# When the tile of probabilities is taken, which banks the transposes use, and which group's scores go first

## The chip, the cores and the metric

One core of a Trainium2 chip runs the kernel. The metric is the device time of one execution in microseconds; the figure of a kernel is the median of its runs. TensorE does the matmuls (row name PE, its weight loads PEld), VectorE (DVE), ScalarE (ACT) and GpSimd (POOL) do the rest, and SyncE (SP) issues most transfers.

## The reference

Three layers one after the other, in float32 (the weights come as 64-bit floats and are unpacked on the chip):

```
def _attn_ref(q, k, v):                    # 4 x 8 heads x 576 x 64
    scores = scale * np.matmul(q, k.transpose(0, 1, 3, 2))
    rel = pos[:, None] - pos[None, :]
    mask = (rel >= 0) & (rel < window)     # window = 64
    scores = np.where(mask, scores, -1000000000.0)
    attn = np.exp(scores - np.max(scores, axis=-1, keepdims=True))
    attn = attn / (np.sum(attn, axis=-1, keepdims=True) + 1e-09)
    return np.matmul(attn, v)

def _moe_ref(x, w_in, w_out):              # 2304 tokens, 512 -> 2048 -> 512
    h = x @ w_in
    return (h * (1.0 / (1.0 + np.exp(-1.702 * h)))) @ w_out

def _moe2_ref(x, w_gate, w_val, w_out, rms_g):   # 512 -> 1536 -> 512
    xn = x / np.sqrt(np.mean(x * x, axis=-1, keepdims=True) + 1e-06) * rms_g
    g = xn @ w_gate
    return (g * (1.0 / (1.0 + np.exp(-g))) * (xn @ w_val)) @ w_out
```

The output is the third applied to the second applied to the attention output, rearranged to 2304 tokens of 512.

## The kernel before

Every operand of the two feed-forward layers is split into a high and a low half that TensorE multiplies in its faster float32 form; three matmuls (high with high, high with low, low with high) stand for one.

**Groups.** Attention works on 36 groups of 64 tokens, all eight heads at once. A group `g` runs: scores on TensorE (`scores`, L428); scale and mask on VectorE into the tile of probabilities `e` (`masked`, L453); the row maximum (L458); exponentials on ScalarE in place, with the row sums (L463); the inverse of the sum (L468, L469); the product with it on GpSimd, in place (`normal`, L472); the transposes of four 128 x 128 blocks on TensorE (`turned`, L477); their copy out of the accumulator into `pt` or `pts` (`turned_out`, through the helper at L312 or L314); the products with v (`values`, L487); and the split of the result into `xh` and `xl` (L312, L494), columns of a ring that the next layer reads. Groups 0 to 7 (`g < NS`) use other tiles and run first. From group 18 (`g >= NPE`) on, VectorE and GpSimd do the transposes instead of TensorE.

**First feed-forward layer.** Six blocks of 512, 256, 384, 384, 384 and 384 tokens. A block runs 16 steps; step c multiplies x with the slab of `w_in` number 2c (the up product, 12 matmuls, L554 to L556), applies the gate with ScalarE (L607) and VectorE (L611), splits the result into `gh` (L312) and `gl` (L569), and multiplies with the slab of `w_out` number 2c + 1 (the down product, 12 matmuls, L628 to L630). In the first block the slabs are made as they are needed: a transfer (L336), ScalarE (L340), three steps on VectorE (L344, L348, L354), a copy as the high half (L312) and a subtraction as the low half (L381). In the program's names the slabs are slab_82 to slab_105, then late_1303 to late_1310: slab_82 is the up slab of step 0, slab_83 the down slab of step 0, slab_84 the up slab of step 1. The groups of attention for a block are spread over the steps of the block before it.

**Second feed-forward layer.** From about 490 us on, products L912 to L914 (with combinations on VectorE, L938) and L1013 to L1015.

**Who decides the order.** Everything is recorded in a `Planner` as operations with costs, priorities, read and written tiles and newly taken buffers (`new=`). `emit` goes through planned time and gives each engine the ready operation with the lowest priority number; where an operation may run on several engines (a subtraction on VectorE or GpSimd, a copy on ScalarE or VectorE), it also decides that. What it emits is each engine's fixed order on the chip. An operation that takes a buffer of a ring waits until the buffer's last user is through. The rings that matter here, in `KINDS`:

```
        "bank": (ps, 2, [P, 512], F32),
        "abank": (ps, 2, [P, 512], F32),
...
        "v": (at, 1, [P, DM], F32),
        "e": (at, 1, [P, NK, P], F32),
        "pt": (at, 1, [P, NK, P], F32),
```

`bank` holds up products; `abank` holds scores, value products and a block's sums; `e` and `pt` are single. `step`, an argument of `attention`, is added to the priority number of a group's transposes and all that follows them; the groups of blocks 2 to 5 stand 13/6 apart in priority, those of block 1 13/4.

Of the kernel before, what the change touches and what calls it, by code (L numbers as in the profile page):

```python
# [189 lines left out]
def act(n, sbuf=True, extra=0):  # L190
    return n / 1200.0 + (0.093 if sbuf else 0.05) + 0.093 * extra


def dve(n, fast=False):
    return n * (0.52e-3 if fast else 1.042e-3) + 0.068
# [11 lines left out]
def window_attention_two_moe_kernel(ctx: ExitStack, tc: tile.TileContext, ins, out):  # L207
# [20 lines left out]
    NPE = gbase[3]  # L228
    NS = ngrp[0]
# [60 lines left out]
    pl = Planner({k: v[1] for k, v in KINDS.items()})  # L290
# [100 lines left out]
    def wkey(g):  # L391
        b, i = divmod(g, NBLK)
        return b, max(i - 1, 0)

    def load_q(g, prio, kind="q"):
        b, i = divmod(g, NBLK)
        t = q_of[g] = Buf(kind)
        pl.op({"D": dma(P * 2048)}, lambda e: nc.sync.dma_start(out=make(t), in_=qh[b, i]), prio, new=[t])

    def load_k(g, prio, kind="k"):  # L400
        if wkey(g) in kw:
            return
        b, i = wkey(g)
        t = kw[b, i] = Buf(kind)
        pl.op({"D": dma(P * 2048)}, lambda e: nc.sync.dma_start(out=make(t), in_=kh[b, :, i:i + 2]), prio, new=[t])

    def load_v(g, prio, kind="v"):
        if wkey(g) in vw:
            return
        b, i = wkey(g)  # L410
        t = vw[b, i] = Buf(kind)
        pl.op({"D": dma(P * 2048)},
              lambda e: nc.sync.dma_start(out=make(t), in_=vh[b, i * W:(i + 2) * W]), prio, new=[t])
# [5 lines left out]
    def attention(g, p0, step, ekind="e", ptkind="pt", norm=("G",), ptev=("A", "V"), hi=("A",)):  # L419
        q, k, v = q_of.pop(g), kw[wkey(g)], vw[wkey(g)]  # L420
        sb, eb, nb, ub, rb = Buf(f"y{g % 3}" if g < NS else "abank"), Buf(ekind), Buf("nm"), Buf("su"), Buf("rc")
        tb, pb, ob = Buf("bank" if g < NS else "abank"), Buf(ptkind), Buf("abank")
        extra = [START] if ekind == "e0" or ptkind == "pt0" or q.kind == "q0" or k.kind == "k0" or v.kind == "v0" else []

        def scores(e):
# [72 lines left out]
        c = (g * W) % RING // W  # L498
        d = step
        if g < NS:  # L500
            pl.op({"T": 1.09}, masked_scores, p0, r=[q, k, "mask", "negative", "ident", *extra],
                  w=[("xh", c), ("xl", c), "scores order"], new=[sb])
            pl.op({"V": dve(512) + 0.1}, highest_of, p0, r=[sb], new=[nb])
            pl.op({"A": 4 * act(128, True, 2)}, powers_of, p0, r=[sb, nb, *extra], new=[ub, eb])
        else:
            pl.op({"T": 0.872}, scores, p0, r=[q, k, *extra], w=[("xh", c), ("xl", c), "scores order"], new=[sb, eb],
                  after=vals[NS - 1:NS] if g >= NS else ())
            pl.op({"V": dve(512)}, masked, p0, r=[sb, "mask"], w=[eb])
            pl.op({"V": dve(512)}, highest, p0, r=[eb], new=[nb])
            pl.op({"A": 4 * act(128, True, 2)}, powers, p0, r=[nb], w=[eb], new=[ub])  # L510
        pl.op({"V": 0.29}, inverse, p0, r=[ub], new=[rb])
# [89 lines left out]
    def a_up(j, c, prio):  # L601
        n = sizes[j]
        hb, o = up("h", lambda: slab_of(2 * c), ("slab", 2 * c), tok0[j], n, prio)
        tb = Buf("th")

        def squash(e):
            nc.scalar.activation(out=make(tb)[:, 0:n], in_=hb.tile[:, 0:n], func=AF.Tanh, scale=0.851)  # L607

        def gated(e):
            th = tb.tile[:, 0:n]  # L610
            nc.vector.scalar_tensor_tensor(out=th, in0=th, scalar=1.0, in1=hb.tile[:, 0:n],  # L611
                                           op0=ALU.add, op1=ALU.mult)

        pl.op({"A": act(n, False)}, squash, prio, r=[hb], new=[tb])
        pl.op({"V": dve(n)}, gated, prio, r=[hb], w=[tb])
        return split(tb, n, prio, tok0[j]), o
# [471 lines left out]
    for g in range(NS):  # L1088
        attention(g, -60 + g, 0.5, "e0" if g >= 2 else ("e", "t1")[g], "pt0" if g % 2 else "pt",
                  norm=("G",) if g < NS - 1 else ("V",))  # L1090
# [14 lines left out]
    order = sorted(range(2 * NA), key=lambda i: need[i])  # L1105
    for i in order:
        c = i // 2
# [18 lines left out]
    def a_down(s):  # L1126
        j, c = steps[s]
        if c == 0:
            accs[j] = [Buf(f"y{m}") for m in range(NK)]
        down_t(accs[j], gates.pop(s), lambda: slab_of(2 * c + 1), ("slab", 2 * c + 1), c == 0, c == NA - 1, sizes[j],  # L1130
               s + LAG)
        if c == NA - 1:
            a_finish(j, accs.pop(j), s + LAG)
# [17 lines left out]
    def b_narrow(i):  # L1151
        (kind, c), src, _ = b_list[i]
        p = n0 + i * (n1 - n0) / len(b_list)
        key = ("w32d", "o", c) if kind == "o" else ("w32d", c - c % 2 + "gv".index(kind), c % 2)
        w_narrow(key, src, p + 8, after=[ups[int(p) - 2]], apart=kind == "o", late=6.0)
        b = w32.pop(key)
        if kind == "o":
            pl.op({"D": dma(P * 2048)}, lambda e: nc.sync.dma_start(out=w32o_d[c], in_=b.tile), p + 8, r=[b], w=[key])
            return
        n = key[1]  # L1160
        if c % 2 == 0:
            halfway[n] = b
            return
        pair = (halfway.pop(n), b)

        def word(h, k, lane):
            return pair[h].tile[:, k * 256:(k + 1) * 256, lane].bitcast(F32)

        for to, x, y, op in (((0, 0), (1, 0, 1), (1, 1, 1), ALU.add), ((0, 1), (0, 0, 0), (0, 0, 1), ALU.subtract),
                             ((1, 0), (0, 0, 1), (1, 0, 1), ALU.subtract), ((1, 1), (0, 1, 1), (0, 1, 0), ALU.subtract)):  # L1170
            xs = [(n, "sum", *v[:2]) for v in (x, y) if v[2] == 0]
            fn = lambda e, to=to, x=x, y=y, op=op: eng[e].tensor_tensor(out=word(*to, 0), in0=word(*x), in1=word(*y), op=op)
            pl.op(both(256), fn, p + 8, r=[*pair, *xs], w=[(n, "sum", *to)], port="GV")
        for h in range(2):
            pl.op({"D": dma(P * 4096)}, lambda e, h=h: nc.sync.dma_start(
                out=w32p_d[n][:, h].bitcast(I32), in_=pair[h].tile), p + 8,
                r=[pair[h], (n, "sum", h, 0), (n, "sum", h, 1)], w=[("w32d", n, h)])
# [4 lines left out]
    for s in range(SA):  # L1182
        j, c = steps[s]
        while pi < len(plans) and plans[pi][0] <= s:
            p, g = plans[pi]
            pi += 1
            load_q(g, p - 4)
            load_k(g, p - 4)
            load_v(g, p - 3)
            attention(g, p - 0.3, 2)  # L1190
        gs, o = a_up(j, c, s)
        ups.append(o)
        gates[s] = gs
        if s - 2 in gates:
            a_down(s - 2)
        while bi < len(b_list) and n0 + bi * (n1 - n0) / len(b_list) <= s:
            b_narrow(bi)
            bi += 1
# [11 lines left out]
    for n in range(NBB * NU):  # L1210
# [4 lines left out]
        if n % 2:  # L1215
            q = n // 2
# [60 lines left out]
```

## Time and profile before

| | |
|---|---|
| runs | 925.57, 926.16 and 928.45 us; median 926.16 us |
| the profiled execution | 925.49 us, with a span of 923.7 us |
| TensorE (PE) busy in the span | 902.2 us, 98% |
| VectorE, ScalarE, GpSimd busy | 647.3, 438.4, 273.2 us |
| granted clock of TensorE, mean | 0.997 |

The span goes from the first to the last instruction of the program; the profiled execution's own time includes what lies around it. Busy shares are averages over stretches that are limited by different things; the rows below are from single stretches. In a row of a timeline stand start, duration, engine, line, operation, written tile <- read tiles, shapes, the number of instructions, and in brackets the idle time before it with what ended it. In a row of waits stand the waiting engine and line, who released it, the total, the number of waits and the longest.

### The profile page before, as it was taken

The numbers are of one execution on the slowest core, as the hardware profiler recorded it, in microseconds if no ns is written. First come the engines' busy times: TensorE is split into PE (matmuls) and PEld (weight loads), VectorE is DVE, ScalarE is ACT, GpSimd is POOL, SyncE is SP. The second block draws the span as 40 slices with busy tenths as digits, with TensorE's granted clock in tenths as the row PEclk, the third lists the DMA queues.
The fourth block names the chain that finished last, engine by engine and source line by source line (L and its number), as shares of the span: only waits on it lengthen the run. The fifth ranks groups of instructions, "written<-read, shape, count | busy, mean of one in ns | idle before, by whom it ended". The sixth has DMA issues, their size and how long they took to land.

```text
span 923.7 us, 15362 instructions
## 1 busy us (share of the span) xinstructions
PE 902.2 (98%) x5436; PEld 835.9 (90%) x5436; DVE 647.3 (70%) x1236; ACT 438.4 (47%) x1081; POOL 273.2 (30%) x387
## 2 busy tenths in 40 slices
PE   8899999999999999999999999999999999999998
PEld 7677789989999999999998989898999999999997
DVE  5999996676767667666467888778667556555553
ACT  6666665566566667565336444443322223322222
POOL 4111012334345342442102622334223225222210
PEclk9999999999999999999999999999999999999999
DMA  8655557665445656543366999888986768966741
GB/s 283 226 174 201 193 188 159 222 206 171 151 147 186 169 183 229 183 160 114 106 231 233 234 359 341 320 280 255 321 236 206 206 201 244 284 205 205 205 144 68
DMA packets 86536, 194.63 MB, mean 211 GB/s; under 512 B 12726, under 2 KB 36027, under 8 KB 84924
## 3 DMA queue, kind: packets, MB, share of 16 engines
q1 hardware_dynamic: 66108, 137.02, 44.5%
q0 software_dynamic: 20352, 56.63, 21.0%
q8 instruction: 43, 0.70, 0.3%
q14 instruction: 33, 0.27, 0.1%
HBM read 140.13 MB, written 53.50 MB: 210 GB/s over the span
## 4 chain that ended last, share of the span: by engine, by line
PE 77%; DVE 12%; DMA 6%; issue 2%; ACT 2%; SPq 0%; POOL 0%; DVEq 0%; ACTq 0%; POOLq 0%
PE bank L912 9%; PE bank L913 9%; PE bank L914 9%; PE y L628 5%; PE y L630 5%; PE y L629 5%; PE bank L554 5%; PE bank L555 5%; PE bank L556 5%; PE y L1013 3%; PE y L1015 3%; PE y L1014 3%; PE abank L428 3%; DVE raw L348 2%; PE abank L487 2%
## 5 line engine op out<-in xcount | busy, mean ns | idle before, releaser
L554 PE MATMUL bank<-xh,slab 128*128 128x384 f32 (+2 forms) x288 | 98.3, 341 | 1.0 <-DVE th L611 1.0
L628 PE MATMUL y<-gh,slab 128*128 128x384 f32 (+2 forms) x288 | 98.5, 342 | 0.5 <-DVE y L653 0.5
L556 PE MATMUL bank<-xh,slab 128*128 128x384 f32 (+2 forms) x288 | 97.0, 337 | 2.0 <-DVE slab L381 2.0
L555 PE MATMUL bank<-xl,slab 128*128 128x384 f32 (+2 forms) x288 | 97.3, 338 | 0.4 <-DVE xl L494 0.3
L630 PE MATMUL y<-gh,slab 128*128 128x384 f32 (+2 forms) x288 | 96.9, 337 | 0.5 <-DVE slab L381 0.5
L629 PE MATMUL y<-gl,slab 128*128 128x384 f32 (+2 forms) x288 | 96.6, 336 | 0.0
L951 ACT ACTIVATE sb<-gh 128x384 f32<-128x384 f32 x72 | 37.8, 525 | 114.0 <-DVE gh L938 114.0
L312 ACT ACTIVATE xh<-sb 128x384 fp32r<-128x384 f32 x72 | 37.1, 521 | 107.5 <-DVE sb L966 107.5
L938 DVE TENSOR_TENSOR gh<-gl,bank 128x384 f32<-128x384 f32 x108 | 59.3, 551 | 35.9 <-PE bank L914 35.1
L611 DVE SCALAR_TENSOR_TENSOR th<-th,bank 128x384 f32<-128x384 f32 (+2 forms) x96 | 52.7, 549 | 42.8 <-ACT th L607 42.3
L913 PE MATMUL bank<-slab,late 128*128 128x384 f32 x228 | 77.0, 338 | 0.0
L913 PE MATMUL bank<-slab,slab 128*128 128x384 f32 x228 | 76.4, 335 | 0.0
L607 ACT ACTIVATE th<-bank 128x384 f32<-128x384 f32 (+2 forms) x96 | 46.7, 486 | 58.1 <-PE bank L556 55.0
L472 POOL TENSOR_TENSOR e<-e,rc 128x512 f32<-128x512 f32 x34 | 37.8, 1111 | 108.9 <-DVE rc L469 102.8
L312 ACT ACTIVATE gh<-th 128x384 fp32r<-128x384 f32 (+2 forms) x96 | 50.2, 523 | 40.3 <-DVE th L611 31.3
L938 DVE TENSOR_TENSOR gl<-gl,bank 128x384 f32<-128x384 f32 x72 | 39.8, 553 | 35.4 <-PE bank L914 31.4
L463 ACT ACTIVATE e<-e,nm 128x128 f32<-128x128 f32 x112 | 43.7, 393 | 33.2 <-DVE nm L458 31.0
L556 PEld LDWEIGHTS bank<-xh,slab 128*128 128x128 f32 x288 | 54.1, 188 | 4.9 <-DVE slab L381 2.8
L554 PEld LDWEIGHTS bank<-xh,slab 128*128 128x128 f32 x288 | 54.1, 188 | 3.6 <-DVE th L611 1.6
L630 PEld LDWEIGHTS y<-gh,slab 128*128 128x128 f32 x288 | 54.1, 188 | 3.2 <-DVE slab L381 1.2
L555 PEld LDWEIGHTS bank<-xl,slab 128*128 128x128 f32 x288 | 54.1, 188 | 3.1 <-DVE xl L494 1.1
L912 PE MATMUL bank<-slab,slab 128*128 128x384 f32 x156 | 53.0, 340 | 3.8 <-ACT th L312 1.7
(198 smaller groups left out, 2596.9 us busy)
## 6 DMA issues: line engine op xcount, KB each, us to landing
slab<-wc POOLq DMA_DIRECT2D x36, 512.0 KB, 4.6
late<-wc POOLq DMA_DIRECT2D x36, 512.0 KB, 4.3
wp<-raw SPq DMA_DIRECT2D x24, 512.0 KB, 4.1
fw<-wp SPq DMA_DIRECT2D x12, 1024.0 KB, 8.1
late<-wo POOLq DMA_DIRECT2D x22, 512.0 KB, 5.5
q<-in_q_dram SPq DMA_DIRECT2D x36, 256.0 KB, 4.4
wc<-slab SPq DMA_DIRECT2D x18, 512.0 KB, 7.1
wc<-late SPq DMA_DIRECT2D x18, 512.0 KB, 5.7
```

The source lines that it names most:

```text
L312: nc.scalar.activation(out=out, in_=in_, func=AF.Copy)
L554: nc.tensor.matmul(h, w[:, 0, kk], xh_ring[:, kk, cols], start=(kk == 0), stop=False)
L555: nc.tensor.matmul(h, w[:, 0, kk], xl_ring[:, kk, cols], start=False, stop=False)
L556: nc.tensor.matmul(h, w[:, 1, kk], xh_ring[:, kk, cols], start=False, stop=(kk == NK - 1))
L611: nc.vector.scalar_tensor_tensor(out=th, in0=th, scalar=1.0, in1=hb.tile[:, 0:n], op0=ALU.add, op1=ALU.mult)
L628: nc.tensor.matmul(y, s[:, 0, cols], hb.tile[:, 0:n], start=first, stop=False)
L629: nc.tensor.matmul(y, s[:, 0, cols], lb.tile[:, 0:n], start=False, stop=False)
L630: nc.tensor.matmul(y, s[:, 1, cols], hb.tile[:, 0:n], start=False, stop=last)
L912: nc.tensor.matmul(h, w[:, 0, kk], xh[:, kk], start=kk == 0, stop=False)
L913: nc.tensor.matmul(h, w[:, 0, kk], xl[:, kk], start=False, stop=False)
L914: nc.tensor.matmul(h, w[:, 1, kk], xh[:, kk], start=False, stop=kk == 1)
L938: nc.vector.tensor_tensor(out=(make(to) if kind else s.tile)[:, 0:HT].bitcast(F32), in0=s.tile[:, 0:HT].bitcast(F32), in1=b.tile[:, 0:HT], ...
```

## The change

For groups from 8 on, three things. The tile of probabilities `e` is taken by the mask step, and no longer by the scores; since `e` is single, the scores of a group no longer wait for the transposes of the group before. The transposes of groups 8 to 17 take their accumulator from `bank`, the ring of two that the up products use, and no longer from `abank`. And `step` is 2.3 where it was 2, so that in the blocks whose groups stand 13/6 apart the next group's scores come ahead of a group's transposes.

```
     def attention(g, p0, step, ekind="e", ptkind="pt", norm=("G",), ptev=("A", "V"), hi=("A",)):
...
-        tb, pb, ob = Buf("bank" if g < NS else "abank"), Buf(ptkind), Buf("abank")
+        tb, pb, ob = Buf("bank" if g < NPE else "abank"), Buf(ptkind), Buf("abank")
...
-            pl.op({"T": 0.872}, scores, p0, r=[q, k, *extra], w=[("xh", c), ("xl", c), "scores order"], new=[sb, eb],
+            pl.op({"T": 0.872}, scores, p0, r=[q, k, *extra], w=[("xh", c), ("xl", c), "scores order"], new=[sb],
                   after=vals[NS - 1:NS] if g >= NS else ())
-            pl.op({"V": dve(512)}, masked, p0, r=[sb, "mask"], w=[eb])
+            pl.op({"V": dve(512)}, masked, p0, r=[sb, "mask"], new=[eb])
...
-            attention(g, p - 0.3, 2)
+            attention(g, p - 0.3, 2.3)
```

The planner then makes another order on every engine from the first of these groups until far into the second layer. Three places of it follow: two of the 512-token block and the 256-token block.

TensorE, the transposes of group 8, early in the 512-token block (`abank<-ident,e` and `bank<-ident,e` are the transposes, `abank<-pts,v` the value products of group 8, slab_86 the third up product, slab_83 the first down product):

```order
 L555 MATMUL bank<-xl,slab_84 128x512
 L556 MATMUL bank<-xh,slab_84 128x512
-L477 MATMUL abank<-ident,e 128x128 x4
+L477 MATMUL bank<-ident,e 128x128 x4
+L628 MATMUL y_710<-gh,slab_83 128x512
+L629 MATMUL y_710<-gl,slab_83 128x512
+L630 MATMUL y_710<-gh,slab_83 128x512
+L487 MATMUL abank<-pts,v 64x64 x8
 L554 MATMUL bank<-xh,slab_86 128x512
 L555 MATMUL bank<-xl,slab_86 128x512
```

The value products and the first three matmuls of the first down product now stand ahead of the third up product; before, both stood behind it.

GpSimd in the same block, before:

```order
L472 TENSOR_TENSOR e<-e,rc 128x512
L381 TENSOR_TENSOR slab_90<-raw,slab_90 128x512
L472 TENSOR_TENSOR e<-e,rc 128x512
L381 TENSOR_TENSOR slab_94<-raw,slab_94 128x512
L569 TENSOR_TENSOR gl<-th,gh 128x512
L472 TENSOR_TENSOR e<-e,rc 128x512
L381 TENSOR_TENSOR slab_99<-raw,slab_99 128x512
L472 TENSOR_TENSOR e<-e,rc 128x512
```

and in the change:

```order
L472 TENSOR_TENSOR e<-e,rc 128x512
L381 TENSOR_TENSOR slab_90<-raw,slab_90 128x512
L472 TENSOR_TENSOR e<-e,rc 128x512
L381 TENSOR_TENSOR slab_96<-raw,slab_96 128x512
L381 TENSOR_TENSOR slab_98<-raw,slab_98 128x512
L472 TENSOR_TENSOR e<-e,rc 128x512
L381 TENSOR_TENSOR slab_97<-raw,slab_97 128x512
L381 TENSOR_TENSOR slab_102<-raw,slab_102 128x512
```

The low halves of slabs 96 and 98 have come to GpSimd, and that of slab 94 has gone to VectorE, with the one split of a gate (L569).

TensorE in the 256-token block: the change puts the scores of groups 13 and 14 on both sides of the value products of group 12, and the transposes of group 14 directly behind the scores of group 15 (`L685` and `L686` are the sums of the block before):

```order
L685 MATMUL abank<-gh,ones 128x512
L686 MATMUL abank<-gl,ones 128x512
L428 MATMUL abank<-k,q 128x128 x4
L487 MATMUL abank<-pts,v 64x64 x8
L428 MATMUL abank<-k,q 128x128 x4
L628 MATMUL y_1654<-gh,slab_87 128x256
```

And six products further on:

```order
L556 MATMUL bank<-xh,slab_94 128x256
L428 MATMUL abank<-k,q 128x128 x4
L477 MATMUL bank<-ident,e 128x128 x4
L554 MATMUL bank<-xh,slab_96 128x256
L555 MATMUL bank<-xl,slab_96 128x256
```

Before, a group's scores stood in this block behind the value products of the group before, with four products or more between a group's scores and its transposes.

At the end of the same block, before (late_1310 is its last down slab, `abank<-k,q` the scores of group 18, `128x384` the first up product of the next block):

```order
L628 MATMUL y_1683<-gh,late_1310 128x256
L629 MATMUL y_1683<-gl,late_1310 128x256
L630 MATMUL y_1683<-gh,late_1310 128x256
L477 MATMUL abank<-ident,e 128x128 x4
L628 MATMUL y_1690<-gh,late_1310 128x256
L629 MATMUL y_1690<-gl,late_1310 128x256
L630 MATMUL y_1690<-gh,late_1310 128x256
L487 MATMUL abank<-pts,v 64x64 x8
L428 MATMUL abank<-k,q 128x128 x4
L554 MATMUL bank<-xh,slab_82 128x384
```

and in the change (late_1306 is the down slab two steps earlier):

```order
L628 MATMUL y_1696<-gh,late_1306 128x256
L629 MATMUL y_1696<-gl,late_1306 128x256
L630 MATMUL y_1696<-gh,late_1306 128x256
L428 MATMUL abank<-k,q 128x128 x4
L554 MATMUL bank<-xh,slab_82 128x384
L555 MATMUL bank<-xl,slab_82 128x384
```

The transposes and value products of group 17 no longer stand here; the transposes now stand ahead of the up product with late_1305, the value products behind it.

## Rows read from the trace of the kernel before

**Rows 1.** Busy time by stretch: length, busy PE, PEld, DVE, ACT, POOL, clock, DMA.
```profile
32.00:130.00 98.00, 94.63 (x479) 74.76 (x480) 93.85 (x165) 63.32 (x131) 12.73 (x10) 1.00 0.55 187
...
187.00:203.00 16.00, 14.25 (x106) 12.81 (x105) 12.63 (x27) 11.25 (x37) 5.00 (x5) 1.00 0.67 223
203.00:424.00 221.00, 220.97 (x1524) 215.08 (x1522) 146.65 (x284) 139.66 (x411) 93.51 (x159) 1.00 0.51 170
```

**Rows 2.** Timeline of TensorE in the 512-token block, five places.
```profile
37.88 0.66 PE L477 MATMUL abank<-ident,e 128*128 128x128 f32 x4 [0.19 <-POOL e L472]
39.03 0.50 PE L554 MATMUL bank<-xh,slab 128*128 128x512 f32 x1 [0.49 <-DVE th L611]
...
45.51 1.05 PE L428 MATMUL abank<-k,q 128*128 128x128 f32 x8
...
55.83 0.50 PE L630 MATMUL y<-gh,slab 128*128 128x512 f32 x1 [0.46 <-DVE slab L381]
...
79.04 0.50 PE L556 MATMUL bank<-xh,slab 128*128 128x512 f32 x1 [1.34 <-DVE slab L381]
```

**Rows 3.** Timeline of VectorE at three places of the first 150 us.
```profile
38.30 0.67 DVE L611 SCALAR_TENSOR_TENSOR th<-th,bank 128x512 f32<-128x512 f32 x1
...
39.84 0.68 DVE L569 TENSOR_TENSOR gl<-th,gh 128x512 fp32r<-128x512 f32 x1
...
41.04 0.68 DVE L611 SCALAR_TENSOR_TENSOR th<-th,bank 128x512 f32<-128x512 f32 x1
...
77.46 1.53 DVE L381 TENSOR_TENSOR slab<-raw,slab 128x512 fp32r<-128x512 f32 x1
...
149.27 0.69 DVE L453 SCALAR_TENSOR_TENSOR e<-abank,m_rest 128x512 f32<-128x512 f32 x1 [0.24 <-PE abank L428]
```

**Rows 4.** Timeline of TensorE in the 256-token block, the starts of six pieces.
```profile
153.31 0.28 PE L628 MATMUL y<-gh,slab 128*128 128x256 f32 x1
...
154.73 0.60 PE L477 MATMUL abank<-ident,e 128*128 128x128 f32 x4
155.09 0.36 PE L554 MATMUL bank<-xh,slab 128*128 128x256 f32 x1
...
156.67 0.69 PE L487 MATMUL abank<-pts,v 128*64 128x64 f32 x16
157.29 1.16 PE L428 MATMUL abank<-k,q 128*128 128x128 f32 x8
158.20 0.36 PE L628 MATMUL y<-gh,slab 128*128 128x256 f32 x1
```

**Rows 5.** Timeline of ScalarE, the copy of group 8's transposes.
```profile
40.59 0.60 ACT L312 ACTIVATE pts<-abank 128x512 f32<-128x512 f32 x1
```

**Rows 6.** Timeline of GpSimd, the normalisation of groups 10 and 13.
```profile
77.13 1.31 POOL L472 TENSOR_TENSOR e<-e,rc 128x512 f32<-128x512 f32 x1 [3.15 <-DVE rc L469]
...
153.25 1.04 POOL L472 TENSOR_TENSOR e<-e,rc 128x512 f32<-128x512 f32 x1 [0.94 <-DVE rc L469]
```

**Rows 7.** Waits of TensorE from 130 to 187 us.
```profile
PE y L628 <- DVE y L653: 0.5, 1, 0.5
```

**Rows 8.** DMA issues: KB each, median us to landing.
```profile
v<-in_v_dram SPq DMA_DIRECT2D x32, 256.0 KB, 3.1
```

**Rows 9.** Waits of TensorE from 187 to 203 us.
```profile
PE bank L554 <- DVE th L611: 0.5, 1, 0.5
PE y L629 <- POOL gl L569: 0.5, 1, 0.5
PE abank L487 <- ACT pts L312: 0.4, 1, 0.4
PE abank L477 <- POOL e L472: 0.3, 1, 0.3
```

**Rows 10.** Waits of TensorE from 424 to 640 us, two of four.
```profile
PE bank L912 <- ACT th L312: 1.7, 1, 1.7
...
PE bank L912 <- DVE th L611: 1.0, 1, 1.0
```

## The prediction

> **What bounds the kernel now.** I read the profile in this order: busy time by stretch, then what TensorE waits for in each stretch, then the timeline around the waits.
>
> The stretches [rows 1] tell three stories. From 32 to 130 us (first layer, 512-token block, weights being unpacked) VectorE is busy 93.85 of 98 us and TensorE 94.63: two engines are full at once, and either can end a wait. From 203 to 424 us TensorE is busy 220.97 of 221: nothing that attention does there can be gained, only lost. Between them, from 187 to 203 us, TensorE is busy 14.25 of 16. That is the place to look at: it is the end of the 256-token block, where the first 384-token block wants x of groups 12 to 17.
>
> Below, S, T and V are a group's scores, transposes and value products on TensorE; U and D with a slab number are a first-layer up product and down product.
>
> **The change part by part.** No matmul and no DMA is added or removed; a few copies and subtractions go to another engine. What changes is what each step may wait for, and so the whole order. I cost it place by place.
>
> *1. T8 (a loss).* Before, T8 runs at 37.88 and U86 at 39.03 [rows 2]. In the change T8 takes a bank of the up products. That ring has two, which U82 and U84 hold, so T8 waits until U82's bank is read, by VectorE's step L611 that ends at 38.30 + 0.67 = 38.97 [rows 3]; VectorE's order is the same up to here in both builds. T8 takes 0.36 [rows 4], so it ends near 39.4. Next stand three matmuls of D83, which need the low half of the first gate, L569, ready at 39.84 + 0.68 = 40.52 [rows 3]. A product of twelve takes 1.42 at 256 columns [rows 4], so 2.84 at 512, and three matmuls 0.71: 40.6 to 41.3. V8 needs ScalarE's copy, done at 40.59 + 0.60 = 41.19 [rows 5]: no wait. V8 takes 0.62 [rows 4], to 41.9; U86's bank (U84's) is free at 41.04 + 0.68 = 41.72 [rows 3], no wait either. U86 2.84 and the nine remaining matmuls of D83 2.1 bring S9 to 46.85, where it stood at 45.51 [rows 2]: **+1.35**.
>
> *2. What the first stretch gives back.* It is full on VectorE too, and the two next waits there are for VectorE: 0.46 at 55.83 and 1.34 at 79.04 [rows 2]. TensorE arriving 1.35 late meets the first one already over. The second is for the low half of slab 98, L381 on VectorE, 77.46 to 78.99; it took 1.53 beside GpSimd's L472, 1.31 from 77.13 [rows 3, 6]. In the change GpSimd makes slabs 96 and 98, and VectorE makes slab 94 and takes group 10's mask and maximum later, so I expect slab 98 before it is asked for. A first matmul after other work lasts 0.36 where one in a run lasts 0.28 [rows 4], so each wait costs 0.1 more than its idle time. Both waits: -(0.46 + 1.34 + 0.2) = **-2.0**. Bounds: nothing (VectorE gives back none of it, its work is as much as before) to all of the stretch's 98 - 94.63 = 3.4 idle [rows 1].
>
> The Trainium skill, "SBUF — State Buffer", section "Who interferes with whom", says that a VectorE instruction with two SBUF inputs and a GpSimd instruction that reads SBUF exclude one another for the whole instruction, so that moving a subtraction to GpSimd frees VectorE of nothing while both run. The 1.53 beside GpSimd's 1.31 agrees. By that rule alone the 79.04 wait stays; that is a rival below.
>
> *3. Evacuation at 141 us.* One wait of 0.5 for VectorE's copy of an accumulator [rows 7]; the change gives three of these four copies to ScalarE and comes to the place one transpose later. I take **-0.5**; bounds -0.6 and 0.
>
> *4. New waits in the 256-token block.* S may now run while the probabilities before it are still in use, so S13, V12 and S14 stand in one row. S14 takes the accumulator bank that the mask step of S13 frees: 0.69 plus 0.24 of handover [rows 3], of which V12 covers 0.62 [rows 4]: +0.3. T14 stands directly behind S15. From the start of a group's mask step to the end of its normalisation is 153.25 + 1.04 - 149.27 = 5.02 [rows 3, 6]. The mask step of group 14 starts when T13 has read the one tile of probabilities; from there to T14 TensorE has U92 1.58, V13 0.62, U94 1.5 and S15 0.91 [rows 4], 4.61: +0.4. T15, T16 and T17 have three to five products between, 1.42 each [rows 4], and wait for nothing. SyncE's queue: the load of v for a group waits for V of the group before (one buffer) and lands in 3.1 [rows 8]; from V13 to V14 lie 1.5 + 0.91 + 0.4 + 0.36 + 1.58 = 4.7, so it is covered by over a microsecond; q and k go two groups ahead. Behind the waiting T14 stand U96 and V14 alone, and their users have slack of a product or more. In all **+0.7**; bounds 0 and +2.0 (each of S14, T13 to T17 waiting about 0.35).
>
> *5. The end of that block.* Before, D, T17, three matmuls of D, V17 and S18 stand in one knot in front of the 384-token block, and TensorE waits 0.5 for GpSimd's low half, 0.3 for GpSimd's normalisation, 0.4 for ScalarE's copy, and 0.5 for the bank of the third up product in a row [rows 9]: all of 187 to 203, 1.75 idle [rows 1]. In the change T17 and V17 stand five and six products earlier, and the up products of the new block alternate with the last down products, so that each bank has a product's time to be read. All four go, with 0.1 of restart each: **-2.1**. Nothing is late next: the x of group 17 is ready before U82.
>
> *6. Beyond 424 us.* The last wait of the first layer, 1.0 for VectorE's L611 at the first product of the second layer [rows 10], now has a down product more in front of it. The rest of the second layer's order on TensorE is the same; its VectorE and GpSimd shares are dealt anew. I take **-0.5**, bounds -2.0 and +2.0.
>
> Between 203 and 424 us I take nothing: TensorE has no idle time to give [rows 1], and a product there is half as long again as in the 256-token block, so the same chain of 5.02 has more cover.
>
> **Sum.** 1.35 - 2.0 - 0.5 + 0.7 - 2.1 - 0.5 = -3.05. The profiled execution took 925.49 us, so 922.4; it lies 0.67 under the median of the runs, 926.16, so I predict a median of **923.1 us**. About 0.3%, 2.8 us, is what a measurement of this kernel can tell from no change, so this is just beyond it. This case by itself spans 920 to 925.5.
>
> **The rivals.**
> *A, slower: the shared bank.* Each of the ten transposed groups puts its T between two up products, so an up product must wait for the gate step of the one right before it. At 38 us the bank came free 4.0 after U84's end (T8 followed it after 0.19 of idle time, so it ended at 37.69 [rows 2]; L611 at 41.72 [rows 3]), while T9 to T11 leave 0.36 + 2.84 + 0.62 = 3.8 between two up products, and T14 leaves 0.91 + 0.36. If the queue of VectorE stays that long everywhere and nothing absorbs item 1, the price is w for each of ten groups. The gains of items 3 and 5 are 2.6, so it is slower by 2.8 from w = 0.54 on. With w = 0.7: 7.0 - 2.6 = +4.4, median 930.6. For it: VectorE is full exactly there. Against: in the 256-token block the gate step is prompt, and the order gives most groups a down product of cover.
> *B, no change:* VectorE alone sets the end of the first stretch (items 1 and 2 come to 0), item 4 is 2.0, items 5 and 3 stay, item 6 is 0: -0.6, median 925.6.
> *C, faster:* the first stretch loses all its 3.4 of idle, and of two waits beyond 424 us (1.7 and 1.0 [rows 10]) 2.5 goes: -3.4 + 0.7 - 0.5 - 2.1 - 2.5 = -7.8, median 918.4.
> *D, the port:* GpSimd's and VectorE's subtractions hold one another up, as at 77.46 [rows 3, 6], and slab 98 is late all the same; item 2 is then -0.56: -1.6, median 924.6. The Trainium skill's rule above would have it so.
> That the scores don't move ahead is no rival: the order shows them ahead in all groups from 12 on.
>
> **How the numbers follow.** Chances: this forecast 0.45 (two thirds of it beyond 0.3%), C 0.13, D 0.10, B 0.16, A 0.16. Faster by over 0.3%: 0.30 + 0.13 + 0.02 = 0.45. Slower: 0.16 and 0.02 from the upper end of B. Same: 0.37. The range 919.0 to 929.0 leaves out the upper part of A (some 0.10) and the lower part of C (some 0.08).
>
> **What would show it.** Right: no wait over 0.2 on TensorE between 180 and 205 us; a wait of about a microsecond at T8 or D83 near 39 to 41; none at the up product of slab 98; waits of 0.3 to 0.5 at S14 and T14. Wrong: waits of TensorE for L611 at up products that follow a T (A); VectorE without idle time in the first stretch and the same total of waits there (B); waits for v's load at V14 or V15; new waits over a microsecond beyond 490 us.

## The result, and the profile after

The change is slower: median 932.64 us (929.03 to 937.19, 13 runs) against 926.46 us (924.15 to 928.48, 13 runs); ratio 1.0065, 95% interval 1.0046 to 1.0083. 923.1 was forecast, 919.0 to 929.0 as its range. The profiled execution took 929.03 us, with a span of 926.8 us: it is the fastest of the 13, and what it shows is less than what the median loses. The figures of e10 below leave out one execution of 1473.17 us, at a mean granted clock of 0.557.

Busy time by stretch, the columns of [rows 1]; first the second stretch of the kernel before, then four stretches of the change:

```profile
130.00:187.00 57.00, 56.49 (x506) 53.98 (x505) 38.95 (x81) 31.29 (x94) 16.00 (x17) 1.00 0.66 193
...
32.00:130.00 98.00, 97.29 (x505) 78.54 (x505) 94.98 (x170) 67.36 (x142) 15.83 (x12) 1.00 0.59 197
130.00:187.00 57.00, 52.29 (x483) 49.42 (x482) 35.69 (x75) 31.20 (x92) 15.25 (x16) 1.00 0.64 187
187.00:203.00 16.00, 15.94 (x113) 15.62 (x113) 11.33 (x24) 10.41 (x33) 5.70 (x11) 1.00 0.49 173
203.00:424.00 221.00, 217.72 (x1500) 211.39 (x1499) 149.47 (x290) 133.57 (x393) 89.75 (x161) 1.00 0.53 169
```

Against [rows 1] the stretch up to 130 us gains 2.66 us (items 1 and 2 had 0.65 together) and that from 187 us gains 1.69 (item 5 had 2.1). The stretch from 130 to 187 us loses 4.20, and the last loses 3.25 where there was nothing idle. TensorE's waits in the second and the last stretch:

```profile
PE abank L487 <- DMA v<-in_v_dram: 2.4, 1, 2.4
PE abank L487 <- ACT e L463: 1.1, 1, 1.1
PE bank L477 <- POOL e L472: 0.9, 2, 0.5
...
PE abank L487 <- DMA v<-in_v_dram: 2.5, 1, 2.5
PE abank L686 <- POOL gl L680: 0.5, 1, 0.5
```

The waits forecast are there and small: S14 0.24, T14 0.41 (its second is T12, 0.45). What is new is L487, the value products, waiting for v. Their places in the timeline of TensorE (V14, V15, and V of group 33):

```profile
159.38 0.34 PE L487 MATMUL abank<-pts,v 128*64 128x64 f32 x4 [2.35 <-DMA v<-in_v_dram]
...
166.89 0.34 PE L487 MATMUL abank<-pts,v 128*64 128x64 f32 x4 [1.10 <-ACT e L463]
...
391.65 0.40 PE L487 MATMUL abank<-pts,v 128*64 128x64 f32 x4 [2.47 <-DMA v<-in_v_dram]
```

V15 is put down to ScalarE's exponentials, with which it has nothing to do; ScalarE's copy of its transposes ran from 164.40 for 0.60, so it was done 1.9 us earlier. That leaves v, by elimination. SyncE's queue shows both loads (L413), with what stands in front:

```profile
147.04 0.86 SPq L1175 DMA_DIRECT2D wp<-raw  x2
...
151.24 0.37 SPq L700 DMA_DIRECT2D rs<-ss  x1
152.08 0.33 SPq L413 DMA_DIRECT2D v<-in_v_dram  x1
152.50 0.38 SPq L336 DMA_DIRECT2D raw<-in_w_val_dram  x1
...
160.09 0.33 SPq L413 DMA_DIRECT2D v<-in_v_dram  x1
```

The load for V14 is issued at 152.08 and V14 starts at 159.38, when it has landed: about 7 us, not 3.1. Just ahead of it stands L700, the store of a block's inverse roots: 2 KB, written as 512 pieces of 4 bytes. Behind it the transfers are slow, though 1.8 MB are issued between 152.08 and 157.15. From 152 to 159 us, the packets and what they moved, and two of the landing times:

```profile
DMA packets 776, 0.64 MB, mean 92 GB/s; under 512 B 557, under 2 KB 557, under 8 KB 775
...
raw<-in_w_val_dram SPq DMA_DIRECT2D x1, 512.0 KB, 9.7
...
q<-in_q_dram SPq DMA_DIRECT2D x1, 256.0 KB, 8.3
```

The kernel before has the same store at 152.34 and the same slow stretch (GB/s from 150 to 162 us in 40 slices; then the landing time of v in that window, its issue, and the value products that use it):

```profile
GB/s 423 141 64 55 143 239 321 389 423 451 403 423 410 209 331 342 341 396 123 55 14 0 27 14 0 27 41 14 20 68 55 0 0 0 21 68 89 164 96 89
...
v<-in_v_dram SPq DMA_DIRECT2D x1, 256.0 KB, 6.8
...
157.40 0.33 SPq L413 DMA_DIRECT2D v<-in_v_dram  x1
...
165.88 0.69 PE L487 MATMUL abank<-pts,v 128*64 128x64 f32 x16
```

There v took 6.8 us, and the value products came 8.5 us after its issue: no wait. In the change V14 could have started 5.0 us after the end of V13 (without its wait), and the same load shows.

The wait at 391.65 is another place: no small store is near (L700 of that block is issued at 370.37). The load of v, issued at 384.51, stands directly behind a load of 512 KB (383.60) and a store of 256 KB (384.03). Two earlier value products, at 226.75 and 232.64, follow the ones in front of them as closely (5.2 us; here 5.3) and do not wait. What makes the load late there is not shown.

### The profile page after: what moved, and what is told of

Its sections match the earlier page's. It is cut to its first block, busy times and chain, and to the rows that moved or that the text cites. A ratio compares the mean times of both kernels' runs of the same rounds, so it can differ in the third digit from the quotient of the medians.

```text
span 926.8 us, 15377 instructions
## 1 busy us (share of the span) xinstructions
PE 902.3 (97%) x5436; PEld 837.0 (90%) x5436; DVE 647.1 (70%) x1235; ACT 435.7 (47%) x1069; POOL 276.4 (30%) x400
## 4 chain that ended last, share of the span: by engine, by line
PE 71%; DVE 11%; DMA 8%; ACT 5%; issue 3%; POOL 1%; SPq 0%; DVEq 0%; ACTq 0%; POOLq 0%
PE bank L912 9%; PE bank L913 8%; PE bank L914 8%; PE y L628 5%; PE bank L554 4%; PE y L630 4%; PE y L629 4%; PE bank L556 4%; PE bank L555 4%; PE y L1013 3%; PE y L1015 3%; PE y L1014 3%; DMA words<-xn 2%; PE abank L428 2%; DMA raw<-in_w_out_dram 2%
## 5 line engine op out<-in xcount | busy, mean ns | idle before, releaser
L611 DVE SCALAR_TENSOR_TENSOR th<-th,bank 128x384 f32<-128x384 f32 (+2 forms) x96 | 52.6, 549 | 57.9 <-ACT th L607 57.8
L629 PEld LDWEIGHTS y<-gl,slab 128*128 128x128 f32 x288 | 54.2, 188 | 2.7 <-DVE gl L569 0.9
L554 PEld LDWEIGHTS bank<-xh,slab 128*128 128x128 f32 x288 | 54.1, 188 | 2.8
L855 POOL DMA_DIRECT2D late<-wc x48 | 27.6, 575 | 95.8 <-PE bank L914 94.0
```

The costliest lines, as they stand in the source:

```text
L554: nc.tensor.matmul(h, w[:, 0, kk], xh_ring[:, kk, cols], start=(kk == 0), stop=False)
L629: nc.tensor.matmul(y, s[:, 0, cols], lb.tile[:, 0:n], start=False, stop=False)
```

## The experiments

A short name for each theory, as the expectations have them: **V**, the single tile of v is what the change waits for; **B**, the shared bank; **C**, the chain from scores to copy; **S**, the small store in front of v. All times are medians, "before" is the kernel before on the same chip. The ratio is worked out from all executions and need not be the quotient of the two medians (for e1 that is 1.0085).

| | us | before | ratio, 95% interval |
|---|---|---|---|
| e1 step back at 2 | 934.99 | 927.14 | 1.0099 (1.0076 to 1.0122) |
| e2 without the banks | 934.58 | 927.14 | 1.0085 (1.0055 to 1.0115) |
| e3 two tiles of v | 928.48 | 927.14 | 1.0019 (1.0001 to 1.0037) |
| e4 planner knows v's load | 926.86 | 927.14 | 0.9998 (0.9979 to 1.0016) |
| e5 no loads of v | 922.83 | 926.47 | 0.9963 (0.9950 to 0.9977) |
| e6 store on GpSimd's queue | 933.32 | 926.47 | 1.0066 (1.0047 to 1.0085) |
| e7 e4 and e6 | 926.55 | 926.47 | 1.0011 (0.9992 to 1.0030) |
| e8 the change again | 933.12 | 926.47 | 1.0082 (1.0057 to 1.0107) |
| e9 before, no loads of v | 925.08 | 926.70 | 0.9975 (0.9963 to 0.9987) |
| e10 stores held back | 930.03 | 926.70 | 1.0037 (1.0017 to 1.0057) |
| e11 e4 and e10 | 932.44 | 926.70 | 1.0055 (1.0034 to 1.0076) |
| e12 before, stores held back | 946.96 | 926.70 | 1.0212 (1.0190 to 1.0235) |
| e13 step 2.3 to group 17 | 931.44 | 926.64 | 1.0048 (1.0031 to 1.0065) |
| e14 first store held back | 930.92 | 926.64 | 1.0044 (1.0028 to 1.0060) |
| e15 e13 and e14 | 926.35 | 926.64 | 0.9997 (0.9981 to 1.0014) |
| e16 e15 and e4 | 932.81 | 926.64 | 1.0060 (1.0039 to 1.0080) |
| e17 load and store in 128 pieces | 920.63 | 926.16 | 0.9944 (0.9923 to 0.9966) |
| e18 e17 and e13 | 920.23 | 926.16 | 0.9944 (0.9925 to 0.9962) |

The tile at the mask alone was not run: with it, every engine's order is that of the kernel before, row for row.

**Which part.** e1 and e2, each undone in the change:

```
-            attention(g, p - 0.3, 2.3)
+            attention(g, p - 0.3, 2)
```
```
-        tb, pb, ob = Buf("bank" if g < NPE else "abank"), Buf(ptkind), Buf("abank")
+        tb, pb, ob = Buf("bank" if g < NS else "abank"), Buf(ptkind), Buf("abank")
```

> The change with step back at 2 (order on every engine the same as with the banks alone). Theory V (the single tile of v: its load is issued only when the value products of the group before are through, and lands up to 7 us later when large transfers move beside it, while step 2.3 puts some value products 4 to 5.5 us apart): the value products stand 5.5 us or more apart, in the 384-token blocks 10 or more, so no wait for v over 0.5 us beyond 203 us; the gains ahead of 130 us stay; median 921 to 925, ratio to before below 1. Theory B (the shared bank costs the time): still slower than before, 929 to 933.

> The change without the banks: tile of probabilities at the mask and step 2.3, transposes in abank. Theory V: value products 5 to 5.5 us apart in five places, so waits for v of 2 us or so in at least two of them, and without what the banks gave ahead of 130 us: 929 to 935, slower than before. Theory B: the loss goes with the banks: 924 to 927.

e2 came out as theory V has it: V14 waits 6.15 us for v at 167.89. It speaks against theory B, too, since without the banks the loss is no smaller. e1 went against theory V: it is as slow, and not by v. TensorE at T13 and T14 of e1:

```profile
151.30 0.33 PE L477 MATMUL bank<-ident,e 128*128 128x128 f32 x1 [3.39 <-POOL e L472]
...
162.80 0.43 PE L477 MATMUL bank<-ident,e 128*128 128x128 f32 x1 [2.09 <-POOL e L472]
```

S13 starts at 145.44 and only one down product lies between it and T13, so the chain of mask, exponentials and normalisation (5.02 in the prediction) is not covered. The banks lose without step 2.3, which keeps the scores well ahead of the transposes, and step 2.3 is what brings the value products together. So with the banks alone it is the chain of theory C that waits, ahead of the transposes, and each of the two loses alone, by another wait.

**Is it v?** e3 gives v two tiles, e4 tells the planner of longer loads, e5 takes the loads away (e9 does it in the kernel before):

```
-        "v": (at, 1, [P, DM], F32),
+        "v": (at, 2, [P, DM], F32),
```
```
-              lambda e: nc.sync.dma_start(out=make(t), in_=vh[b, i * W:(i + 2) * W]), prio, new=[t])
+              lambda e: nc.sync.dma_start(out=make(t), in_=vh[b, i * W:(i + 2) * W]), prio, new=[t],
+              late=4.0 if kind == "v" and prio > 0 else 0.0)
```
```
-              lambda e: nc.sync.dma_start(out=make(t), in_=vh[b, i * W:(i + 2) * W]), prio, new=[t])
+              lambda e: fetch_v(t, b, i, prio), prio, new=[t])
...
+        if prio > 0 and first_v: t.tile = first_v[0]
```

> The change with two tiles of v instead of one. The room comes from the start (v0 has two instead of three), the masks (bfloat16 copies) and the ones (32 columns instead of 128, so the block's sums fill 32 partitions). The order moves a little; value products still stand 4 to 5.5 us apart in places. Theory V: no wait for v at all from 130 to 424 us, 923 to 926. Theory C (the chain of scores, mask, exponentials, normalisation, transposes, copy is what is late, v only comes last by chance): other waits at the same value products take its place, 929 to 932.

> The change with the planner told that a load of v takes 4 us more (a number that only sets the order; rings and transfers stay). Value products stand 7.5 us or more apart but for one place at 5.0. Theory V: at most one wait for v, 923 to 927. Theory C: the waits at value products go on elsewhere or turn into waits at transposes, 928 to 932.

> The change, order of all engines kept, without the loads of v for groups 9 to 35: their value products read the v of group 8 (so the values of those groups are not the reference's). Theory V: no wait for v, none of the drops of granted clock behind it; the gains of the first stretch and of the knot remain: 921 to 924. Theory C (another link of the chain is as late as v): waits at the same value products for the copy of the transposes; 927 or more.

> The kernel before, order of all engines kept, without the loads of v for groups 9 to 35 (those groups read the v of group 8, so their values are not the reference's). Theory V: before, the value products stand 6.9 us or more apart and no wait for v is in its trace, so nothing is to be had: 925 to 927.5, same as before. Rival T (less traffic helps any version: 27 transfers of 256 KB): 922 to 924, and the gain without the loads in the change was no proof.

e5 is decisive: with every order kept, 10.3 us go (933.12 to 922.83), and from 130 to 187 us only two waits of TensorE are left:

```profile
PE bank L477 <- POOL e L472: 0.4, 1, 0.4
PE abank L428 <- DVE e L453: 0.2, 1, 0.2
```

e9 is the control. (e5 and e9 keep 9 of the 32 loads of v, the last near 42 us; so 23 transfers are taken away, not 27, and it is groups 11 to 35 that read an older v.) In the kernel before the same loads cost 1.6 us by the medians and 1.2 to 3.4 by the interval, though it never waits for them there, so part of rival T holds. If they cost the change by their traffic as much as the kernel before, 8.7 us are left that v costs the change alone. The rest of the change gives 922.83 - 926.47 + 1.6 = -2.0 us, where the sum had -3.05. e3 and e4 get most of it back. e3 is slower than V said (1.3 over before); its start is another one, and what it waits for instead is not settled. In e4 V14 still waits 1.59, though it could have started 9.1 us after the end of V13.

**The change again.**

> The change itself, a second profile. The first profile was the fastest of 13 runs (929.03 against a median of 932.64), with granted clock 0.998, while the others had 0.990 to 0.998. Theory V with the clock: in an execution nearer to the median the wait for v is longer than 2.4 us and the granted clock falls for some microseconds behind it; time 930 to 935. Rival: the clock falls somewhere else, away from the waits for v.

The wait at V14 is longer here, and the granted clock falls. TensorE at V14, and busy time in pieces of 4 us:

```profile
163.02 0.37 PE L487 MATMUL abank<-pts,v 128*64 128x64 f32 x2 [3.95 <-DMA v<-in_v_dram]
```
```profile
156.00:160.00 4.00, 2.58 (x21) 2.19 (x20) 2.54 (x6) 2.20 (x8) 1.71 (x2) 1.00 1.07 49
160.00:164.00 4.00, 0.98 (x16) 0.96 (x16) 0.35 (x2) 0.95 (x6) 1.04 (x1) 0.65 0.68 116
164.00:168.00 4.00, 4.00 (x21) 3.93 (x19) 1.18 (x3) 1.07 (x3) 0.00 (x0) 0.50 0.87 336
168.00:172.00 4.00, 4.00 (x46) 3.87 (x46) 2.04 (x4) 2.09 (x5) 0.75 (x1) 1.00 0.25 77
```

From 164 to 168 us TensorE is busy all the time and gets 21 matmuls done where the next piece has 46: the clock is at 0.50, 1.2 of 2.4 GHz, after the idle time. So a wait for v can be paid twice. In the first profile (2.35 us of wait) the clock stayed at 1.00, which fits its being the fastest.

**Is it the store?** e6 issues it from GpSimd, e10 holds it back:

```
-            nc.sync.dma_start(out=rs_d[j].rearrange("one (t p) -> p (one t)", p=P), in_=cb.tile[:, 0:n // P])
+            nc.gpsimd.dma_start(out=rs_d[j].rearrange("one (t p) -> p (one t)", p=P), in_=cb.tile[:, 0:n // P])
```
```
-        pl.op({"D": 0.45}, back, prio, r=[cb], w=[("rs", j)])
+        backs.append(lambda after: pl.op({"D": 0.45}, back, prio + 6, r=[cb], w=[("rs", j)], after=after))
...
             attention(g, p - 0.3, 2.3)
+            while g + 1 in gbase and backs: backs.pop()(vals[-1:])
```

> The change with one transfer per block, the store of the inverse roots (2 KB and less in pieces of 4 bytes), issued by GpSimd on its own queue instead of SyncE. TensorE's, VectorE's and ScalarE's orders stay. In the traces so far 1 us to 4 us after this store (152 us) the transfers of SyncE's queue move 14 to 90 GB/s for several microseconds with 256 to 800 KB waiting, and v behind it lands after 7 us. Theory Q (the store holds up what stands behind it in its queue): v of group 14 lands in 3 to 4 us, the wait at 159 us goes, the one at 392 us stays: 926 to 929. Rival D (the 16 DMA engines are held up by the small pieces whatever the queue): the wait at 159 us stays, 930 to 934.

> The change with the planner told that v takes 4 us more, and the small store on GpSimd's queue. Theories V and Q together: no wait for v over 0.5 us; 922 to 925, faster than before by 0.2 to 0.5%. If only V holds: as the one without the store moved, 927.

> The change, with the store of the inverse roots of a block held back until the value products of the last group of the block that runs beside it, where the next value products are 22 us away (before: about 9 us after the sums, in the middle of the groups). TensorE's order stays. Theory S (this store of 512 pieces of 4 bytes keeps all transfers slow for several microseconds, whatever its queue): the wait at 159 us (group 14) falls to under 1 us, that at 392 us stays at 0 to 2.5: 925 to 928. Rival W (the two stores of 512 KB in front of v, issued at 147 us, are what v waits behind): the wait stays at 2 to 4 us, 930 to 934.

> The change with the planner told that v takes 4 us more, and the store of the inverse roots held back. Theories V and S: no wait for v over 0.5 us, no fall of the granted clock between 130 and 203 us, 922 to 925 and faster than before. Rival W: a wait of 1 to 2 us at the value products of group 14 stays, 926 to 928.

> The kernel before with the same store held back alone: no wait for v was there to lose. Theory V: same as before within 0.3%, 925 to 928. If it is faster than 924, the store costs the kernel before something that its waits don't name.

e6 went as rival D said. V14, the transfers from 158 to 166 us, and the queue of the store in that window:

```profile
165.24 0.69 PE L487 MATMUL abank<-pts,v 128*64 128x64 f32 x16 [3.42 <-DMA v<-in_v_dram]
...
DMA packets 366, 0.88 MB, mean 110 GB/s; under 512 B 64, under 2 KB 64, under 8 KB 366
...
q0 software_dynamic: 32, 0.00, 0.6%
```

Issued from another engine, the store holds up SyncE's transfers all the same. (The Trainium skill, "DMA: Bandwidth & Descriptors", section "Issuing engines are not separate DMA queues", says that transfers started by ScalarE, SyncE or GpSimd run on the same 16 DMA engines in the end; the row agrees.) On GpSimd's queue the profile has the store as 32 packets, not as 512 pieces, so what it is in the store's form that holds the others up is not shown. e7 is e4 within its interval.

e10 has no wait at V14 in its profile. With every order on TensorE the same and the two stores of 512 KB still in front of v, its transfers from 152 to 159 us have a mean of 286 GB/s (the last number of the row), where the change has 92:

```profile
152.00:159.00 7.00, 6.59 (x76) 6.00 (x74) 4.05 (x10) 4.23 (x17) 1.87 (x3) 1.00 0.82 286
```

So rival W is out as the cause of the slow stretch, and so is the load of the block's means (L697), which has the same 512 pieces and stays where it was. The median is not what S said (930.03, in W's range). There is a wait of 1.76 for v at 389.65, and the profile is again the fastest execution (925.14), so what the others lose is not shown. e11 and e12 were wrong for all theories: the store now stands where a block ends (issued at 194.35 in e11). There the stretch behind it is slow, 25 GB/s in e11, where the kernel before has 366. The rows from 198 to 203 us, first e11, then the kernel before:

```profile
198.00:203.00 5.00, 5.00 (x33) 5.00 (x32) 3.79 (x8) 3.24 (x12) 1.04 (x1) 1.00 0.39 25
...
198.00:203.00 5.00, 4.46 (x26) 4.14 (x26) 3.10 (x7) 3.99 (x14) 3.21 (x3) 1.00 1.03 366
```

What waits for it in e11, on TensorE, on ScalarE and on SyncE's queue:

```profile
209.07 0.69 PE L628 MATMUL y<-gh,slab 128*128 128x384 f32 x1 [3.98 <-ACT sq L657]
...
208.27 0.47 ACT L650 ACTIVATE y<-y,gcol 128x256 f32<-128x256 f32 x1 [6.44 <-DMA xn<-y]
...
SPq L336 <- DMA wp<-raw: 8.3, 1, 8.3
```

The stores of the block's results (`xn<-y`, L660) land late. ScalarE, which needs the tile of such a store for the next result (L650), stands for 6.44 us, and TensorE then waits for the accumulators that ScalarE reads (L650, L657). SyncE stands as well: it waits 8.3 us until an earlier store of 512 KB has landed, before it may load into that store's tile. e12 has three waits of TensorE at the ends of blocks, 4.84, 4.96 and 5.39 us, with the clock at half for 6 to 7 us at each; in front of each VectorE waits 5.6 to 9.0 us for a store of the results to land.

**How it splits, and both mended.** e13 has `2.3 if g < NPE else 2` for the step, e14 holds back the store of block 0 alone, e15 and e16 join them.

> The change with step 2.3 for the groups up to 17 only and 2 from group 18 on: from there the value products stand 11.3 us or more apart, in the 256-token block 4.0 to 8.3 as in the change. Theory V: the wait of 2.4 to 4 us at the value products of group 14 and the fall of the granted clock stay, no wait for v beyond 203 us; of the 10 us some 3 to 4 come back: 928 to 931. Rival G (nearly all is lost in the 256-token block): 931 to 934.

> The change with the store of the inverse roots of the first block alone held back until the value products of group 17. Theory V: no wait for v in the 256-token block, in the 384-token blocks one or two of up to 2.5 us: 926 to 929. If it is 930 or more, as with all stores held back, the 384-token blocks cost more in most executions than in the profiles seen.

> Both: step 2.3 up to group 17 only, and the store of the first block held back. Theory V: no wait for v over 0.5 us anywhere, no fall of the granted clock after 40 us; as without the loads of v, plus the 1.6 us that those loads cost the kernel before by their traffic: 923 to 925.5, faster than before. If it is 927 or more, something else in the 256-token block takes the gains.

> As the last, with the planner told besides that v takes 4 us more, so that the value products of the 256-token block stand 6.9 us or more apart. Theory V: same as the last or 1 us less, 922.5 to 925. If the last is slow by v and this is not, the spacing of 4.0 us was still too little without the store in front.

Against before on the same chip, the change stands at +6.7 (e8), e13 at +4.8, e14 at +4.3, e15 at -0.3. So taking away either place gives some 2 us, which the intervals do not tell from nothing (e13 lies in rival G's range), and taking away both gives 7, which is clear of them. e13 shows the first alone, V14 waiting 6.62 at 164.87, and the clock at 0.50 behind it; e14 still waits 1.9 for v at 393 us and has a wait at a block's end:

```profile
203.06 0.69 PE L628 MATMUL y<-gh,slab 128*128 128x384 f32 x1 [3.83 <-DVE y L653]
```

e15 has 2.8 us of the same and misses its 923 to 925.5. e16 waits 4.3 us there, and is as slow as the change. In all three the results' stores land late again. In e16 the small store stands in front of them (194.29), as in e11; in e14 and e15 it was issued some 15 us earlier, at 181.34 and 181.50, and why they are late there is not shown. So moving the store brought a new wait each time. e17 and e18 leave it in place and change its form, and that of the load before it (L697):

```
-            nc.sync.dma_start(out=rs_d[j].rearrange("one (t p) -> p (one t)", p=P), in_=cb.tile[:, 0:n // P])
+            nc.sync.dma_start(out=rs_d[j].rearrange("one (p t) -> p (one t)", p=P), in_=cb.tile[:, 0:n // P])
```

> The change, with the block's means and inverse roots taken to and from the 128 partitions as one piece of 16 bytes for each partition (8 and 12 in the later blocks) instead of four of 4 bytes; which partition raises which mean to the power does not matter. All orders stay. Theory S (the number of pieces is what holds up the transfers behind): no wait for v over 1 us in the 256-token block, no fall of the granted clock there, the 384-token blocks as before: 925 to 929. Rival W (the stores of 512 KB ahead of v are the cause): the wait of 2.4 to 4 us stays, 930 to 934.

> The same with step 2.3 up to group 17 only. Theory S: no wait for v over 0.5 us anywhere and none at a block's end: 922.5 to 925, faster than before by 0.2 to 0.4%. Rival W: as the change with step 2.3 up to group 17 alone, 930 to 932.

With all orders those of the change, e17 is 12.5 us faster than e8, 920.63, and faster than the kernel before by 0.56% (0.34 to 0.77%). Both are faster than their expectations, 925 to 929 and 922.5 to 925, so theory S had the sign and the wait, and its size too small. The waits of e17 from 130 to 187 us, and the landing of the load of 512 KB behind its store:

```profile
PE bank L477 <- POOL e L472: 0.4, 1, 0.4
PE abank L428 <- DVE e L453: 0.2, 1, 0.2
PE y L628 <- ACT y L650: 0.2, 1, 0.2
...
raw<-in_w_val_dram SPq DMA_DIRECT2D x1, 512.0 KB, 5.0
```

e18 is the same within the intervals, with one wait of 0.8 us at a block's end. Its store is issued at 151.71; the transfers from 152 to 159 us, beside the 0.64 MB of the change, and its stretches:

```profile
DMA packets 765, 1.54 MB, mean 221 GB/s; under 512 B 206, under 2 KB 206, under 8 KB 764
...
v<-in_v_dram SPq DMA_DIRECT2D x2, 256.0 KB, 4.0
```
```profile
32.00:130.00 98.00, 97.01 (x504) 78.19 (x504) 94.59 (x172) 67.45 (x143) 15.85 (x12) 1.00 0.62 198
130.00:187.00 57.00, 56.15 (x513) 53.41 (x512) 37.91 (x81) 32.60 (x95) 15.27 (x16) 1.00 0.57 189
187.00:203.00 16.00, 15.24 (x101) 14.79 (x99) 11.29 (x23) 10.59 (x33) 6.44 (x12) 1.00 0.52 181
203.00:424.00 221.00, 221.00 (x1523) 215.26 (x1523) 147.89 (x290) 136.82 (x403) 87.71 (x150) 1.00 0.51 173
```

v lands in 4.0, and the second and last stretch have back what the change lost (the last one by the step as well; e17, whose step is that of the change, has 220.08 there and no wait for v at all from 203 to 424 us). No small store stands near the change's wait at 391.65, so why that wait is gone too is not shown. The form of the store in the kernel before was not run. How much of the 5.5 us is the form alone stays open: the rest of the change is worth 2.0 by e5 and e9, and before has no wait for v to lose.

## Why the prediction was wrong, step by step

*Item 4, the step that failed.* "The load of v for a group ... lands in 3.1 [rows 8]; from V13 to V14 lie ... 4.7, so it is covered by over a microsecond." 3.1 is the median of 32 loads over the whole program. In this stretch a load took 6.8 already before, and about 7 in the change, behind the small store. The wait of zero in the sum was 2.35 in the fastest execution, 3.95 with the clock at half behind it in one nearer to the median, 6.62 in e13. The prediction named waits for v at V14 or V15 as a sign of being wrong, but gave them no price and no chance. The other waits of item 4 were right: 0.24 and 0.41 for 0.3 and 0.4.

*"Between 203 and 424 us I take nothing"* failed by the same load: value products come as close as 5.2 us there, where step 2 leaves 11.4 (e13). I had only asked whether the chain of 5.02 is covered. The stretch lost 3.25.

*Items 2, 3 and 5 were right in their mechanism.* The only wait from 32 to 130 us is one of 0.60 at D83, so rival D's, for slab 98, did not come; items 1 and 2 together gave -2.66 in the profiled execution, for -0.65. Of the 0.5 at 141 us 0.15 is left. The end of the block gave -1.7 for -2.1. *Item 6* came to nothing in sum, within its bounds: TensorE is busy 0.71 longer from 424 to 490 us and 0.75 shorter from 490 to 915 (419.58 after 420.33), where -0.5 was forecast.

*Item 1 was mis-sized in the profiled execution:* T8 did not wait, D83 0.60, and S9 came at 45.26, where 46.85 was forecast. In others of the same order on TensorE it was there: T8 waits 1.87 in e6, 2.17 in e17. It is one of the things in which executions differ.

*Rival A* had the sign and not the mechanism: no up product waits for L611 behind a T in the traces of the change. The clock was in none of the rivals.

What the other terms came to is shown by e5: without the waits for v the change takes 922.8, beside 923.1 forecast, but 1.6 of that is traffic left out. With it, 924.4: the rest of the sum had the right sign and was about a microsecond too large.

## What to carry to other kernels

The landing time of a transfer is that of its place: read it there, with what stands ahead on the queue, not as a median over the program. Where a reorder brings two users of a single buffer closer, its refill is on the path from then on, and each of its waits can cost again in the clock. A tiny transfer in many pieces can hold up everything behind it; here another form helped, and another place or another issuing engine did not.

## What was not expected of the hardware

Behind a store of 2 KB in 512 pieces of 4 bytes the transfers of 7 us had a mean of 92 GB/s; without the store there the mean is 286 (e10), and where the store is moved the slow stretch follows (25 GB/s in e11). Issued by GpSimd it held them too (e6, 110 GB/s), though there it shows as 32 packets. In 128 pieces of 16 bytes the mean is 221 (e18), and the load of 512 KB behind it lands in 5.0 (e17) instead of 9.7 us.

Waits of TensorE of 3.39 (e1), 3.95 (e8), 6.15 (e2) and 6.62 us (e13) ended in or were followed by the clock at 0.50; so were those of 2.09 (e1) and 1.99 (e6, at 173.68), while 2.35 (the change) and 3.42 (e6) were not. Length alone does not decide it in these traces. The kernel before has such a stretch near its start too, 24 to 28 us:

```profile
24.00:28.00 4.00, 3.47 (x45) 2.81 (x47) 3.96 (x11) 2.72 (x6) 0.00 (x0) 0.59 0.70 243
```

It lasts to 35 us in e8 and is missing in e18, so it is one of the things in which profiled executions differ. How much of the 3 to 6 us by which a profile here may lie from its kernel's median it makes up was not measured.
